# Attention and token mixer on one core: q loaded in 6 KB rows, transposes in row tiles, evictions shared by two engines

## The chip, the cores and the metric

The kernel runs on one core of one Trainium2 chip. The metric is the device time of one execution in microseconds. Before the change the median of three runs was 222.12 us (221.69 to 222.29). Runs of the same kernel come in a fast and a slower state; only fast runs are compared here, and one execution of each kernel carries the profile.

## The reference, cut to what matters

Grouped-query attention (16 query heads, 4 key/value heads, 384 positions, head width 64, 8 batches) followed by a mixer over the positions. Inputs and output are 32-bit floats; the kernel computes in bf16.

```python
k = np.repeat(k, group, axis=1); v = np.repeat(v, group, axis=1)     # group = 4
attn = softmax((1/np.sqrt(D)) * q @ k.transpose(0, 1, 3, 2))
x = (attn @ v).transpose(0, 2, 1, 3).reshape(B, S, H * D)            # 8 x 384 x 1024
wq, wk = x @ w_q, x @ w_k                                            # 64 wide
W_tok = (1/np.sqrt(64)) * np.einsum('bsd,btd->bst', wq, wk)
out = np.maximum(np.einsum('bst,btd->bsd', W_tok, x), 0.0) @ w_out   # 8 x 384 x 1024
```

## The kernel before

A builder writes all engines' instructions in one pass. It keeps estimated clocks for TensorE, VectorE and ScalarE, and at each step it takes the piece of work that those clocks say is ready. What it emits is fixed: if an estimate is wrong, an engine waits.

Per batch: q, k and v are loaded, cast to bf16 on GpSimd, transposed (by TensorE for batches 0 and 1, by DMA afterwards), multiplied to scores, exponentiated on ScalarE and multiplied by v. Then x is transposed and goes through the mixer and the output projection. Positions are dealt out as position = 3 * partition + c, so an output block c of 128 partitions is a store with one stride:

```python
def ld(dst, src, a, z, c0=0, c1=C):                     # C = 3: rows of 3 x 64 floats = 768 bytes
    nc.sync.dma_start(out=dst[:, a:z, c0:c1],
                      in_=src[b, a:z].rearrange("h (p c) d -> p h c d", p=P)[:, :, c0:c1])
...
def x_tr(b, c):                                         # eight 128 x 128 transposes
    ...
    for dc in range(DC):
        nc.tensor.transpose(out=ps[:, dc, :], in_=xn[:, c, dc * P:(dc + 1) * P], identity=ident)
    nc.vector.tensor_copy(out=xTs[b][:, :, c, :], in_=ps)
...
def po():                                               # output projection, one matmul a call
    ...
    osb = osbs[b, c]
    dst = out[b].rearrange("(p c) n -> c p n", c=C)[c]  # 128 rows of 4 KB, one every 12 KB
    ...
        nc.vector.tensor_copy(out=osb[:, n0:n1], in_=ps[:, n0 - half * NH:n1 - half * NH])
    ...
    if half == 1 and not last:
        nc.sync.dma_start(out=dst, in_=osb)             # 512 KB
```

The last store of all is cut into one of 256 KB and two of 128 KB. There are 26 stores in the program.

The softmax here doesn't subtract the row's maximum and nothing guards it: scores larger than these inputs give would overflow.

## Time and profile before

| | before |
|---|---|
| median of the three runs | 222.12 us |
| the profiled execution | 226.12 us, span 224.3 us |
| TensorE busy | 95% of the span |
| last copy of the output ends | 221.54 us in the profile |
| from there to the end | 2.8 us |

Most lines of this profile are in the prediction below. Five more: the shares of the chain that ended last; the DMA queue with its packets, megabytes and share of 16 engines' time; the score matmuls, with busy time, mean ns, and the idle time before them and what ended most of it; and two lines of the DMA issues with count, size and the median time from issue to landing.

```profile
PE 74%; DMA 14%; DVE 3%; SPq 3%; POOL 3%; issue 1%; DVEq 0%
...
q1 hardware_dynamic: 71520, 45.62, 77.6%
...
L259 PE MATMUL sc<-QT,KT 64*128 64x512 bf16 x288 | 47.5, 387 | 3.1 <-DMA QT<-qb 2.9
...
out_dram<-osb SPq DMA_DIRECT2D x23, 512.0 KB, 3.1
...
QT<-qb SPq DMA_TRANSPOSE x18, 3.7
```

Windows: time between the marks, busy time of each engine with the count of instructions, granted TensorE clock, share of the 16 DMA engines (the times of their packets added up, so that it can pass 1), and GB/s.

```profile
215.00:221.50 6.50, 5.74 (x27) 2.41 (x25) 2.80 (x5) 0.00 (x0) 0.00 (x0) 1.00 0.51 202
221.50:224.30 2.80, 0.00 (x0) 0.00 (x0) 0.04 (x1) 0.00 (x0) 0.00 (x0) 1.00 0.28 94
```

The reader is to keep two things: a store lands in 3.1 us, and after the last copy only 2.8 us go by, in which 94 GB/s x 2.8 us = 0.26 MB leave the core.

### The profile page before, as it was taken

The numbers are of one execution on the slowest core, as the hardware profiler recorded it, in microseconds if no ns is written. First come the engines' busy times: TensorE is split into PE (matmuls) and PEld (weight loads), VectorE is DVE, ScalarE is ACT, GpSimd is POOL, SyncE is SP. The second block draws the span as 40 slices with busy tenths as digits, with TensorE's granted clock in tenths as the row PEclk, the third lists the DMA queues.
The fourth block names the chain that finished last, engine by engine and source line by source line (L and its number), as shares of the span: only waits on it lengthen the run. The fifth ranks groups of instructions, "written<-read, shape, count | busy, mean of one in ns | idle before, by whom it ended". The sixth has DMA issues, their size and how long they took to land.

```text
span 224.3 us, 5470 instructions
## 1 busy us (share of the span) xinstructions
PE 214.2 (95%) x2217; PEld 113.6 (51%) x2244; DVE 145.2 (65%) x365; ACT 140.6 (63%) x146; POOL 52.1 (23%) x97
## 2 busy tenths in 40 slices
PE   8999999589999999999999999999999999999993
PEld 5666665245545545454555546554555553434441
DVE  2355786834697758865887648874679569576332
ACT  3599998747788778887887887887888600000000
POOL 1385678406300540045016100620000000000000
PEclk9999999959999999999999999999999999999999
DMA  6996999999399979999999998989224422242424
GB/s 174 324 327 170 410 386 325 136 237 323 65 183 215 335 166 187 222 338 216 223 229 342 154 213 260 281 205 154 99 91 53 143 93 93 93 190 93 180 101 187
DMA packets 71688, 46.09 MB, mean 205 GB/s; under 512 B 42736, under 2 KB 67568, under 8 KB 71664
## 3 DMA queue, kind: packets, MB, share of 16 engines
q1 hardware_dynamic: 71520, 45.62, 77.6%
q8 instruction: 17, 0.28, 0.5%
q10 hardware_dynamic: 144, 0.13, 0.2%
q14 instruction: 7, 0.06, 0.1%
HBM read 23.59 MB, written 12.58 MB: 161 GB/s over the span
## 4 chain that ended last, share of the span: by engine, by line
PE 74%; DMA 14%; DVE 3%; SPq 3%; POOL 3%; issue 1%; DVEq 0%
PE bank L408 37%; PE bank L282 13%; PE sc L259 12%; DMA qraw<-in_q_dram 12%; PE bank L331 4%; SPq L129 3%; PE bank L384 3%; PE bank L362 2%; DMA QT<-qb 2%; PE bank L322 1%; POOL qb L158 1%; DVE osb L421 1%; PE bank L349 1%; DVE msb L389 1%; POOL wqk_sb L596 1%
## 5 line engine op out<-in xcount | busy, mean ns | idle before, releaser
L263 ACT ACTIVATE pt<-sc 128x1024 bf16<-128x1024 f32 x144 | 138.9, 1023 | 34.6 <-PE sc L259 34.4
L408 PE MATMUL bank<-wout_sb,msb 128*128 128x512 bf16 x357 | 91.7, 382 | 1.3 <-issue 0.5
L408 PEld LDWEIGHTS <-msb 128*128 128x128 bf16 x384 | 33.8, 98 | 42.4 <-issue 13.7
L259 PE MATMUL sc<-QT,KT 64*128 64x512 bf16 x288 | 47.5, 387 | 3.1 <-DMA QT<-qb 2.9
L282 PEld LDWEIGHTS <-pt 128*128 128x128 bf16 x1152 | 41.9, 98 | 15.8 <-issue 9.9
L282 PE MATMUL bank<-vext,pt 128*128 128x65 bf16 x1152 | 46.9, 195 | 0.4 <-DVE osb L421 0.2
L421 DVE COPY osb<-bank 128x512 f32<-128x512 f32 (+1 forms) x49 | 33.1, 677 | 21.7 <-PE bank L408 20.5
L289 DVE TENSOR_TENSOR xnat<-bank,rcp 128x256 bf16<-128x256 f32 x96 | 40.8, 425 | 3.3
L389 DVE TENSOR_SCALAR msb<-bank 128x384 bf16<-128x384 f32 x64 | 32.5, 551 | 9.5 <-PE bank L384 9.0
L287 DVE RECIPROCAL rcp<-bank 128x4 f32<-128x4 f32 x96 | 16.9, 176 | 17.6 <-PE bank L282 16.7
L158 POOL CAST qb<-qraw 128x768 bf16<-128x768 f32 x30 | 24.0, 827 | 17.4 <-DMA qraw<-in_q_dram 15.1
L153 POOL CAST kb<-kraw 128x192 bf16<-128x192 f32 x30 | 9.2, 347 | 67.3 <-DMA kraw<-in_k_dram 67.3
L259 PEld LDWEIGHTS <-KT 64*128 64x128 bf16 x288 | 12.4, 94 | 24.1 <-issue 17.2
L117 PE MATMUL bank<-idle 128*128 128x256 bf16 x80 | 14.8, 324 | 1.0 <-DVE idle L562 1.0
L331 PE MATMUL bank<-xT,wqk_sb 128*128 128x384 bf16 x64 | 11.7, 327 | 0.0
L117 PEld LDWEIGHTS <-idle 128*128 128x128 bf16 x80 | 7.9, 114 | 6.6 <-issue 4.0
L384 PE MATMUL bank<-wT,Csb 64*128 64x384 bf16 x32 | 10.6, 332 | 0.4 <-DVE rcp L287 0.3
L384 PE MATMUL bank<-wq,Csb 64*128 64x384 bf16 x32 | 10.6, 332 | 0.0
L599 POOL CAST wout_sb<-wld 128x1024 bf16<-128x1024 f32 x8 | 8.1, 1040 | 4.1 <-DMA wld<-in_moe_w_out_dram 4.1
L366 DVE CAST Csb<-bank 128x512 bf16<-128x512 f32 x8 | 5.5, 688 | 5.2 <-PE bank L362 5.2
L337 DVE CAST wT<-bank 128x384 bf16<-128x384 f32 x8 | 4.5, 558 | 6.7 <-PE bank L331 6.7
L323 DVE COPY xT<-bank 128x1024 bf16<-128x1024 bf16 x10 | 6.9, 688 | 2.5 <-PE bank L322 2.5
(33 smaller groups left out, 70.1 us busy)
## 6 DMA issues: line engine op xcount, KB each, us to landing
out_dram<-osb SPq DMA_DIRECT2D x23, 512.0 KB, 3.1
qraw<-in_q_dram SPq DMA_DIRECT2D x15, 768.0 KB, 7.4
wld<-in_moe_w_out_dram SPq DMA_DIRECT2D x4, 1024.0 KB, 9.5
kraw<-in_k_dram SPq DMA_DIRECT2D x7, 384.0 KB, 4.3
vraw<-in_v_dram SPq DMA_DIRECT2D x7, 384.0 KB, 8.9
qraw<-in_q_dram SPq DMA_DIRECT2D x1, 512.0 KB, 5.3
kraw<-in_k_dram SPq DMA_DIRECT2D x2, 192.0 KB, 3.7
vraw<-in_v_dram SPq DMA_DIRECT2D x2, 192.0 KB, 6.3
```

The source lines that it names most:

```text
L117: nc.tensor.matmul(out=bank_ps[i][:, :256], lhsT=idle[:, :P], rhs=idle, start=True, stop=True)
L158: eng.tensor_copy(out=nats[b][1][:, :, kp, :, u, :].rearrange("p c i d -> p i c d"), in_=raws[b][2][:, h0:h0 + G])
L259: nc.tensor.matmul(out=ps[:, u, :], lhsT=KT[lo:hi, kp * C + kc, :], rhs=QT[lo:hi, t0:t0 + G, :].rearrange("k i p -> k (i p)"), start=True, ...
L263: nc.scalar.activation(out=pt.rearrange("k u i p -> k u (i p)"), in_=ps, func=AF.Exp, scale=attn_scale)
L282: nc.tensor.matmul(out=ps[:, i * DE:i * DE + D + 1], lhsT=tiles[kc][:, u, i, :], rhs=vext[:, 2 * kp + u, kc, :D + 1], start=(kc == 0), sto ...
L287: nc.vector.reciprocal(out=rcp, in_=avv[:, :, D])
L289: nc.vector.tensor_tensor(out=xnats[b][:, c, h0:h0 + G, :], in0=avv[:, :, :D], in1=rcp.to_broadcast([P, G, D]), op=ALU.mult)
L331: nc.tensor.matmul(out=ps, lhsT=wqk_sb[:, dc, :], rhs=xT[:, dc].rearrange("d c p -> d (c p)"), start=(dc == 0), stop=(dc == DC - 1))
L384: nc.tensor.matmul(out=bank_ps[i][:, :S], lhsT=Csb[lo:hi, j * P:(j + 1) * P], rhs=w[lo:hi, :], start=True, stop=True)
L389: nc.vector.tensor_scalar_max(out=msb[:, dc, :], in0=bank_ps[i][:, :S], scalar1=0.0)
L408: nc.tensor.matmul(out=ps, lhsT=msbs[b][:, dc, c * P:(c + 1) * P], rhs=wout_sb[:, dc, half * NH:(half + 1) * NH], start=(nd == 0), stop=(n ...
L421: nc.vector.tensor_copy(out=osb[:, n0:n1], in_=ps[:, n0 - half * NH:n1 - half * NH])
```

## The change

Intent: (1) load q in rows of 6 KB, that is 24 positions of a head, in place of 768 bytes, and get batch 2 ready earlier; (2) do each 128 x 128 transpose on TensorE as two row tiles of 64 rows that run side by side; (3) let the builder's clocks choose VectorE or ScalarE for each copy out of PSUM in the projection and relu; (4) reckon DMA and GpSimd times in the builder too. A partition now holds position = 24 * s + 8 * c + m, so the output store gets another pattern. The core of the diff, cut:

```diff
+    M = 8
+    def evac(dst, src, end, ns_dve, ns_act, relu=False, act=True):
+        late = max(clk["act"], end + 200) + ns_act + MARG
+        if act and late < max(clk["dve"], end + 200) + ns_dve:
+            ...                              # ScalarE: activation Relu, or copy
+        ...                                  # else VectorE
 ... 
-            ld(kraw, k, 0, 4)
-            ld(qraw, q, 0, half)
-            ld(qraw, q, half, Hq)
+            src = q[b].rearrange("(u a) (s t) d -> (a s) u t d", u=2, t=C * M)
+            nc.sync.dma_start(out=qraw[:, :, c0 * M:c1 * M], in_=src[:, :, c0 * M:c1 * M])
 ...
+    def half_trs(srcs):
+        for j, src in enumerate(srcs):
+            for half in range(2):
+                lo, hi = half * H, (half + 1) * H
+                nc.tensor.transpose(out=outs[half][:, j, :], in_=src[lo:hi], identity=ident[lo:hi, lo:hi])
 ...
-            nc.vector.tensor_scalar_max(out=msb[:, dc, :], in0=bank_ps[i][:, :S], scalar1=0.0)
-            ready["M", b, dc] = bank_free[i] = on("dve", 560, end)
+            ready["M", b, dc] = bank_free[i] = evac(msb[:, dc, :], bank_ps[i][:, :S], end, 560, 500, True, True)
 ...
-        dst = out[b].rearrange("(p c) n -> c p n", c=C)[c]
+        dst = out[b].rearrange("(s c m) n -> c m s n", c=C, m=M)[c]
 ...
-            nc.vector.tensor_copy(out=osb[:, n0:n1], in_=ps[:, n0 - half * NH:n1 - half * NH])
+            done = evac(osb[:, n0:n1], ps[:, n0 - half * NH:n1 - half * NH], end,
+                        180 + (n1 - n0), 150 + (n1 - n0) * 0.86, False, True)
 ... (start of the program, order of the first casts, load and casts of batch 2 ahead, x of batch 1 transposed by TensorE and no longer by DMA: cut)
```

The store moves the same 128 rows of 4 KB. As an access pattern it was 128 x 1024; it is now 8 x 16 x 1024.

## The prediction

> **What bounds the kernel now**
>
> I read the page first (busy time, slices), then one table of windows, then the chain of waits, then the timeline where the chain leaves TensorE.
>
> From the page of the kernel before, the slices and three groups:
>
> ```profile
> PE   8999999589999999999999999999999999999993
> ACT  3599998747788778887887887887888600000000
> ...
> PEclk9999999959999999999999999999999999999999
> DMA  6996999999399979999999998989224422242424
> ...
> L263 ACT ACTIVATE pt<-sc 128x1024 bf16<-128x1024 f32 x144 | 138.9, 1023 | 34.6 <-PE sc L259 34.4
> ...
> L117 PE MATMUL bank<-idle 128*128 128x256 bf16 x80 | 14.8, 324 | 1.0 <-DVE idle L562 1.0
> ...
> L322 PE MATMUL bank<-ident,xnat 128*128 128x128 bf16 x80 | 6.1, 220 | 0.0
> ```
>
> TensorE is 90% or more busy in nearly every slice, with one dip near slice 8, where its clock also dips. DMA is full until slice 27. Busy is not useful, though: 80 of the matmuls are fillers on a dummy tile (L117), put in where the builder expected a wait. So I cut the span by phase:
>
> ```profile
> core 0: us, PE busy (x) PEld busy (x) DVE busy (x) ACT busy (x) POOL busy (x), PEclk, DMA share, GB/s
> 0.00:7.10 7.10, 6.06 (x33) 4.20 (x33) 1.82 (x7) 1.69 (x2) 0.91 (x10) 1.00 0.76 204
> 7.10:25.00 17.90, 17.90 (x229) 11.54 (x228) 9.26 (x27) 16.34 (x18) 11.37 (x21) 1.00 0.94 288
> 25.00:35.00 10.00, 10.00 (x152) 6.28 (x150) 7.79 (x21) 9.13 (x10) 6.91 (x7) 1.00 1.04 389
> 35.00:43.20 8.20, 7.47 (x109) 4.16 (x107) 6.78 (x21) 8.11 (x9) 6.34 (x12) 1.00 1.19 220
> 43.20:51.50 8.30, 5.97 (x42) 2.80 (x45) 3.12 (x8) 3.42 (x4) 0.72 (x3) 0.59 1.09 242
> 51.50:177.00 125.50, 123.36 (x1428) 65.47 (x1449) 89.95 (x236) 100.84 (x104) 25.87 (x48) 1.00 0.86 204
> ```
>
> Three regimes. Up to 7.1 us nothing useful can run: the first scores wait for K and q. From 7 to 43 us ScalarE sets the pace (16.34 of 17.9 us busy): 36 exponentials of two batches, one by one. From 43.2 to 51.5 us everything is slack: the granted clock is 0.59, VectorE is busy 3.12 of 8.3 us. From 51.5 us TensorE is the bound.
>
> The chain of waits gives what one instruction costs when they follow each other:
>
> ```profile
> 24.88 14.96 DMA qraw<-in_q_dram
> 39.90 1.60 POOL qb L158 x2
> 41.53 3.79 DMA QT<-qb
> 45.45 0.61 PE sc L259 x2
> ...
> 70.21 0.75 PE bank L282 x24
> ...
> 72.47 0.45 PE bank L322 x8
> ...
> 74.74 1.31 PE bank L331 x8
> ...
> 203.15 8.74 PE bank L408 x40
> ```
>
> The upper part says why 43 to 45 us is empty: batch 2's q was asked for at 24.88 us, arrived at 39.8, was cast, transposed by DMA, and the scores of batch 2 start only at 45.45. The lower part gives pitches: attention 31 ns, a 128-wide transpose 56 ns, projection of x 164 ns, output projection 218 ns.
>
> With these pitches I checked that 51.5 to 170 us has no slack. By source, it holds 100 pairs of score matmuls (x 0.216), 792 attention matmuls (x 0.031), 196 output-projection weight loads (x 0.216), 48 L331, 48 L322, and 18, 15 and 18 of the mixer's pairs and transposes: 21.6 + 24.8 + 42.3 + 7.8 + 2.7 + 7.2 = 106.4 of 118.5 us. The other 12.1 us over 50 bursts of scores is 0.24 us a burst, which is the change into two-row tiling and back. So there a microsecond of TensorE work taken out is a microsecond of time, and nothing else is.
>
> **What the Trainium skill says**
>
> "TensorEngine Tiling (Array Packing)", Key Properties: changing the tiling mode drains TensorE, and tiles run weight loads and matmuls in parallel. The trace agrees with both: 0.24 us a burst above, and four score matmuls of two tiles take 0.61 us together with their four weight loads starting within 0.11 us (timeline).
>
> "TensorE: Matmul & The Clock Gate", Part 1: an idle stretch of some 3.4 us halves the clock until a busy one follows. The trace has one such dip: 2.9 us idle before 45.45, then 0.59 in the window. The single profiled execution took 226.12 us against a median of 222.12, so I take most of the low clock to be this execution's.
>
> "ScalarE: Activation LUTs", What ACT_TABLE_LOAD costs: 186 ns + 0.833 ns an element with immediate scale. That gives 1039 ns for the exponential (measured 1023), so a 128x512 eviction on ScalarE should be about 0.61 us (estimate); VectorE's takes 0.688 us in the trace.
>
> "DMA: Bandwidth & Descriptors", Why a DMA increments its semaphore by 16 and not by 1: a DMA runs on the largest number of engines up to 16 that divides the slowest dimension of both sides. The new output pattern has 8 as its slowest DRAM dimension, so stores may use 8 engines. No run here shows it yet.
>
> **The change part by part**
>
> q in 6 KB rows. A q load of the kernel before is 768-byte runs (256 and 512 bytes for the first). The row becomes 24 consecutive sequence rows of a head, 6 KB. In the windows the queue moved 288 GB/s with q, k and v and 389 GB/s with the weights in 4 KB rows, both with the engines full. 4.7 MB of q for batches 0 to 2 at 389 instead of 288 GB/s: 16.3 - 12.1 = 4.2 us (estimate). Loads and casts of batch 2 also move ahead in program order, behind the weights. Batch 2's q would be there near 36 us; six casts of some 0.5 us and a transpose by DMA (3.7 us to landing) put its first scores near 41 to 42 us, when ScalarE is done with the 36 exponentials. The hole closes. Its worth: 2.9 us idle, 11 fillers (1.4 us) and about 0.41 x 8.3 = 3.4 us of lost clock are 7.7 us in the profiled execution; the timed runs are 4.0 us shorter, so some 3.7 us are left in them. I count 3.0.
>
> Start. ScalarE has holes of 1.06 us at 10.4 and 0.89 us at 34.1, and the first scores wait from 5 to 7.1 us behind a transpose placed by a fixed time and 7 fillers. The new order (all heads of one block, clocks from estimated loads) removes most of this; but q's first piece is 512 instead of 256 KB, and the cast is twice as long. I count 1.0 us.
>
> Row-tiled transposes. Each 128x128 transpose becomes two of 64 rows that run at once, 64 columns wide: at the attention's pitch (65 columns, 31 ns) about 30 ns for the pair instead of 56. x: before 10 blocks of 8, 10 x 0.45 = 4.5 us; after 12 blocks (batch 1 leaves the DMA), 12 x 0.24 = 2.8 us: -1.7 us. The small transposes of wk: 8 x (0.165 - 0.09) = -0.6 us. K and q of batches 0 and 1: 60 x 26 ns = 1.6 us, but these lie in ScalarE's regime and become fillers: I count 0.3. VectorE pays two copies of 0.42 instead of one of 0.69, 0.15 us x 12 = 1.8 us, while it has 28% of its time free: nothing.
>
> ScalarE or VectorE for evictions. VectorE is 72% and ScalarE 80% busy from 51.5 to 177 us, and TensorE was shown to be full. So this frees banks sooner, which almost nobody waits for: 0 there. After 177 us ScalarE is empty, but VectorE is only 56% busy and the forty output projections at 218 ns each show no wait: 0. The last block's two quarter copies (0.42 us each) can go to two engines: -0.35 us.
>
> Output stores. Rows stay 4 KB. If 8 engines carry them, the last 128 KB takes longer by about the time of its bytes, estimated +0.35 us; before that, 512 KB every 3.5 us fits. The two cancel.
>
> Fewer mode changes. x and wk transposes join the row-tiled burst, and tiled steps wait up to 2.0 instead of 1.2 us for the next burst. Most already sat in bursts: 0.
>
> Sum: 3.0 + 1.0 + 1.7 + 0.6 + 0.3 = 6.6 us; 222.1 - 6.6 = 215.5 us.
>
> **Rivals**
>
> The hole moves, not closes. DMA is full until 45 us with the same bytes; if 6 KB rows run no faster, batch 2's q arrives no sooner and the scores still wait. For it: share near 1.0 also when it moved 389 GB/s. Against: that rate itself shows long rows moving more. It would leave 219.
>
> Row tiles don't overlap for short matmuls. If two weight loads per transpose serialise, a pair costs 60 ns: x then costs 12 x 0.48 = 5.8 us instead of 2.8. Against: weight loads of score pairs start together. It would make 218.5.
>
> ScalarE becomes the bound. Evictions of 0.6 us in front of an exponential delay a burst, and TensorE, in fixed order, waits. ScalarE can take some 20% before it is full; the output projection alone is 48 x 0.61 = 29 us. The builder gives VectorE 0.1 us of preference. For a loss: the order comes from estimated clocks, and an error makes waits. It would add 1 to 3 us.
>
> Score matmuls slow down. They now read q in runs of 16 elements with a step between instead of whole rows. If the stream lost 10%, 144 pairs x 22 ns = 3.2 us. No line speaks to it.
>
> More gain than counted: with output projection able to start at about 32 us instead of 49.8 us, the timed runs may recover more than 3.7 us; 212 to 213.
>
> **Range and chances**
>
> The sum's solid part is 2.3 us of transposes; the 4.0 us of the hole and start rest on estimates of DMA, worth 1 to 7. Hence 211.5 to 219.5. Faster by 2% means below 217.7 us: needs two thirds of the sum less a bit, 0.72. Within 2%: 0.25. Slower: needs two rivals at once and no gain, 0.03.
>
> **What would show it**
>
> Right: no idle of TensorE above 1 us after the first scores, PEclk without a dip, output projection starting before 36 us, q loads landing sooner, eight x transposes in 0.24 us in the chain, 12 blocks. Wrong: scores of batch 2 waiting on DMA at 42 us; a pair of half transposes at 56 ns or more; score pairs above 0.23 us; TensorE waiting for ScalarE's evictions or gaps between bursts in 51 to 177 us; a store taking well over 3.1 us to land at the end. Should the fillers of the first 25 us grow by what the transposes save, that part was rightly counted as nothing.

## The result, and the profile after

| | before | after |
|---|---|---|
| median | 222.2 us (221.69 to 224.82, 4 runs) | 232.85 us (231.71 to 234.0, 4 runs) |
| ratio of fast runs | | 1.0454 (95%: 1.0347 to 1.0562), slower |
| span of the profiled execution | 224.3 us | 229.9 us |

A ratio here is the mean time of one kernel's fast runs over that of the other's of the same rounds, so it is not quite the ratio of the medians quoted.

The change costs 10.7 us where 6.6 us of gain had been predicted. The page of the changed kernel, with the lines that answer to those above:

```profile
PE   5999999999999997999999989999599999999950
...
PEclk9799999999999999999999999999889999999996
DMA  6999998939997999989999999999944293344542
...
q1 hardware_dynamic: 54232, 45.10, 84.4%
...
PE 47%; DMA 29%; SPq 5%; ACT 5%; issue 4%; POOL 4%; DVE 1%; POOLq 0%; DVEq 0%; ACTq 0%
...
L294 PE MATMUL sc<-QT,KT 64*128 64x512 bf16 x288 | 47.8, 385 | 5.8 <-DMA QT<-qb 4.2
...
out_dram<-osb SPq DMA_DIRECT2D x23, 512.0 KB
```

The chain's share of TensorE fell from 74% to 47%, and that of DMA rose from 14% to 29%. The queue carries a quarter fewer packets (54,232 for 71,520) and nearly as many bytes, and yet holds the engines longer (84.4% for 77.6%). TensorE has two new dips, in slices 16 and 29 of 40, and the last slice is empty. For the stores the page gives no landing time at all: that field is missing from all its transfers. The chain of waits, middle part (start, length, what):

```profile
82.05 9.05 DMA QT<-qb
...
108.45 5.78 DMA QT<-qb
...
120.19 13.83 DMA vraw<-in_v_dram
...
141.16 12.03 DMA qraw<-in_q_dram
...
156.57 7.46 DMA QT<-qb
...
164.16 0.61 PE sc L294 x4
```

These are links that the chain before did not have after 46 us. The three transposes of q by DMA on this chain take 5.8 to 9.1 us to land; before, the slowest of all 18 took 5.2 us, and the median was 3.7. TensorE waits for it at 91, 114 and 164 us. The windows of the changed kernel:

```profile
7.10:25.00 17.90, 17.71 (x314) 11.12 (x313) 10.95 (x38) 15.96 (x17) 12.92 (x22) 0.90 1.07 372
...
51.50:177.00 125.50, 120.02 (x1384) 62.63 (x1383) 79.78 (x216) 95.62 (x105) 23.84 (x52) 0.99 1.00 195
```

```profile
215.00:222.30 7.30, 6.36 (x30) 2.65 (x28) 0.42 (x1) 2.20 (x5) 0.00 (x0) 1.00 0.50 152
222.30:229.90 7.60, 0.00 (x0) 0.00 (x0) 0.00 (x0) 0.00 (x0) 0.00 (x0) 0.77 0.32 106
```

From 51.5 to 177 us the DMA share is 1.00 (0.86 before) for fewer GB/s (195 for 204), and TensorE is idle for 5.5 us of it (120.02 busy). The 123.36 of the kernel before is no fair measure for this, since its trace lacks 21 matmuls in this window (1,428 for 1,449 weight loads); that of the changed kernel lacks none. At the end there are 7.6 us after the last copy, in which 106 GB/s x 7.6 us = 0.81 MB leave: a store and a half was still to go, where before it was half a store. Just before that, the share stands at 0.50 for 152 GB/s, where before it stood at 0.51 for 202. The trace's single packets tell the two apart: in the changed kernel seven or more are in flight all through this window, and just eight for 6.05 of its 7.30 us. In the kernel before, from 200 us to the last copy, it is none for 11.9 of 21.5 us, and sixteen for 6.1.

The trace has one direct count of how many engines take part: its packets of 4 bytes. There are 2,289 of them before, which is sixteen for each of 67 copies, thirty-two for each of 38 transposes by DMA, and one more. In the changed kernel there are 1,889. With its stores turned back to a pattern of 16 (below) it is 2,097: 208 fewer in the changed kernel, which is 26 stores x 8. So each store ran on 8 engines in place of 16.

The landing times that the page leaves out can be had from the trace's semaphore updates by transfers. There are 1,338, which is nine for each of the 26 stores and sixteen for each of the 69 other transfers. Counted off in the order of issue, the stores take 5.9 to 12.0 us to land (median 7.1; before 1.7 to 8.2, median 2.9), and the transposes of q 3.1 to 9.4 us (median 4.2).

### The profile page after: what moved, and what is told of

Read it like the earlier page. It is cut to its first block, busy times and chain, and to the rows that moved or that the text cites. A ratio compares the mean times of both kernels' runs of the same rounds, so it can differ in the third digit from the quotient of the medians.

```text
span 229.9 us, 5881 instructions
## 1 busy us (share of the span) xinstructions
PE 212.3 (92%) x2409; PEld 110.5 (48%) x2409; DVE 126.7 (55%) x350; ACT 158.0 (69%) x180; POOL 53.3 (23%) x110
## 3 DMA queue, kind: packets, MB, share of 16 engines
q1 hardware_dynamic: 54232, 45.10, 84.4%
## 4 chain that ended last, share of the span: by engine, by line
PE 47%; DMA 29%; SPq 5%; ACT 5%; issue 4%; POOL 4%; DVE 1%; POOLq 0%; DVEq 0%; ACTq 0%
PE bank L441 21%; DMA qraw<-in_q_dram 10%; DMA QT<-qb 10%; DMA vraw<-in_v_dram 9%; PE sc L294 8%; PE bank L319 8%; ACT pt L299 4%; PE bank L145 3%; POOL qb L197 3%; PE bank L365 2%; SPq L234 2%; PE bank L397 1%; PE bank L251 1%; PE bank L418 1%; SPq L176 1%
## 5 line engine op out<-in xcount | busy, mean ns | idle before, releaser
L299 ACT ACTIVATE pt<-sc 128x1024 bf16<-128x1024 f32 x144 | 139.4, 1024 | 38.0 <-PE sc L294 37.6
L441 PE MATMUL bank<-wout_sb,msb 128*128 128x512 bf16 x384 | 96.0, 382 | 0.0
L441 PEld LDWEIGHTS <-msb 128*128 128x128 bf16 x384 | 33.1, 98 | 43.5 <-issue 13.3
L117 DVE TENSOR_SCALAR msb<-bank 128x384 bf16<-128x384 f32 x54 | 27.8, 552 | 15.9 <-PE bank L418 15.7
L197 POOL CAST qb<-qraw 128x512 bf16<-128x512 f32 x45 | 25.9, 619 | 21.9 <-DMA qraw<-in_q_dram 13.1
L119 DVE COPY osb<-bank 128x512 f32<-128x512 f32 (+1 forms) x25 | 16.9, 678 | 24.6 <-PE bank L441 24.3
L114 ACT COPY osb<-bank 128x512 f32<-128x512 f32 (+1 forms) x24 | 13.9, 577 | 19.1 <-PE bank L441 17.4
L145 PE MATMUL bank<-idle 128*128 128x256 bf16 x73 | 13.9, 324 | 1.0 <-DVE idle L617 1.0
L257 DVE COPY xT<-bank 128x512 bf16<-128x512 bf16 x24 | 9.1, 419 | 8.6 <-PE bank L251 8.5
L145 PEld LDWEIGHTS <-idle 128*128 128x128 bf16 x73 | 6.9, 112 | 5.8 <-issue 3.0
```

The costliest lines, as they stand in the source:

```text
L117: nc.vector.tensor_scalar_max(out=dst, in0=src, scalar1=0.0)
L119: nc.vector.tensor_copy(out=dst, in_=src)
L145: nc.tensor.matmul(out=bank_ps[i][:, :256], lhsT=idle[:, :P], rhs=idle, start=True, stop=True)
L197: copy(out=nats[b][1][:, c * M:(c + 1) * M, u, :], in_=raws[b][2][:, u, c * M:(c + 1) * M])
L299: nc.scalar.activation(out=pt.rearrange("k u i p -> k u (i p)"), in_=ps, func=AF.Exp, scale=attn_scale)
L441: nc.tensor.matmul(out=ps, lhsT=msbs[b][:, dc, c * P:(c + 1) * P], rhs=wout_sb[:, dc, half * NH:(half + 1) * NH], start=(nd == 0), stop=(n ...
```

## The experiments

Theory, after the traces: the store's pattern puts it on 8 of the 16 engines. These 8 also carry their share of every load and transpose, and those have landed only when the slowest of their engines is done. The DMA was already nearly full, so transposes come late in the middle, and stores pile up at the end. Rivals: the evictions on ScalarE, put in order by wrong clocks (R1); the scattered order of the rows in DRAM, not the engines (R2); the new loads and transposes, so that the stores only show it (R3).

One warning on correctness: in this reference the rows of a batch are almost alike; rolling them by one position changes the output by 1.3% (relative norm). A store to wrong rows is therefore still told correct. Kernels 2, 3, 5, 9, 11 and 12 put rows in wrong places. The changed kernel, 1, 4, 6, 7, 8 and 10 put them in the right ones by construction.

### 1 to 3: the store's pattern alone

Run 1 keeps everything of the change, but the relu writes its positions in another order, so that the store's outermost dimension is 16. The Trainium skill advises this on "DMA: Bandwidth & Descriptors", Rules for kernel authors: the engines are set by the outermost dimension, which should be a multiple of 16.

```diff
-            ready["M", b, dc] = bank_free[i] = evac(msb[:, dc, :], bank_ps[i][:, :S], end, 560, 500, True, True)
+            ready["M", b, dc] = bank_free[i] = evac(
+                msb[:, dc, :].rearrange("p (c s m) -> p c s m", c=C, m=M),
+                bank_ps[i][:, :S].rearrange("p (c m s) -> p c s m", c=C, m=M), end, 560, 500, True, True)
-        dst = out[b].rearrange("(s c m) n -> c m s n", c=C, m=M)[c]
+        dst = out[b].rearrange("(s c m) n -> c s m n", c=C, m=M)[c]
```

> The changed kernel with the output stores on a pattern whose slowest DRAM dimension is 16 instead of 8 (the relu copies write the rows in that order; right result). Theory S (stores on 8 engines cost both the 4.9 us longer tail and the late transposes of q): tail after the last copy back to about 3 us from 7.6, waits of TensorE on QT near 0, time 213 to 218. Rival T (stores cost only the tail): 227 to 228, waits on QT stay near 4 us. Rival A (clocks and evictions make the waits): as T.

Run 2 keeps the change and takes the old store pattern (wrong rows).

```diff
-        dst = out[b].rearrange("(s c m) n -> c m s n", c=C, m=M)[c]
+        dst = out[b].rearrange("(p c) n -> c p n", c=C)[c]
```

> The changed kernel with only the DRAM rows of the stores changed to those of the kernel before (3 rows apart, one merged dimension of 128); the rows land in the wrong places on purpose. No on-chip instruction differs. Theory S: same as the 16-engine version within 1 us, 213 to 218. Rival T or A: 227 to 228. If this one is fast and the right 16-engine version is not, the permuted relu write is what costs.

Run 3 puts the new store pattern into the kernel before (wrong rows).

```diff
-        dst = out[b].rearrange("(p c) n -> c p n", c=C)[c]
+        dst = out[b].rearrange("(s c m) n -> c m s n", c=C, m=8)[c]
```

> The kernel before with only the DRAM pattern of the stores of the change (slowest dimension 8); wrong places on purpose. Theory S: stores on 8 engines cost here too, tail +4 to +5 us and some waits on QT: 227 to 233. Rival T: about 227. Rival A (the loss is in the change's on-chip part): 222 to 223.

| run | median us | ratio to before (95%) |
|---|---|---|
| 1, change with 16-wide store | 220.42 (219.94 to 221.63) | 0.989 (0.9837 to 0.9944) |
| 2, change with the old store pattern | 219.38 (219.32 to 220.81) | 0.9851 (0.98 to 0.9902) |
| 3, kernel before with 8-wide store | 246.22 (245.97 to 248.97) | 1.1067 (1.0993 to 1.1142) |

The store's pattern is the loss: 232.85 - 220.42 = 12.4 us in the changed kernel, and 246.22 - 222.84 = 23.4 us in the kernel before, which has nothing else of the change. R3 is out. The line of the score matmuls and what they wait for, on the page of run 3:

```profile
L259 PE MATMUL sc<-QT,KT 64*128 64x512 bf16 x288 | 47.9, 391 | 16.3 <-DMA QT<-qb 16.1
```

The same on the page of run 1:

```profile
PE 88%; ACT 5%; issue 2%; DMA 2%; DVE 1%; SPq 0%; DVEq 0%
...
L294 PE MATMUL sc<-QT,KT 64*128 64x512 bf16 x288 | 47.5, 387 | 0.9 <-ACT pt L299 0.3
...
out_dram<-osb SPq DMA_DIRECT2D x23, 512.0 KB, 4.6
```

The wait for the transposed q is gone from run 1 and more than five times the kernel before's 2.9 us in run 3. I had expected run 3 to lose 5 to 11 us; it lost twice as much and more. Runs 1 and 2 missed their range too (213 to 218), by 2.4 and 1.4 us: what the change gains without the loss is less than predicted. Run 2's stores land in 2.9 us and run 1's in 4.6, without a difference in time beyond the intervals: the landing time of a store alone does not tell what it costs.

### 4: the evictions on ScalarE

```diff
-        if act and late < max(clk["dve"], end + 200) + ns_dve:
+        if False and late < max(clk["dve"], end + 200) + ns_dve:
```

> The changed kernel with every eviction on VectorE again, stores still on 8 engines. Theory S: within 1.5 us of the changed kernel, 231 to 234. Rival A (evictions on ScalarE delay exponentials and make the waits): 227 to 229, with the waits of the score matmuls on ScalarE and QT gone.

Measured: 233.35, 234.45 and 235.10 us in its fast runs (a fourth, 238.21, is slow), ratio 1.0526 (1.0456 to 1.0596). Its page still has the wait:

```profile
L294 PE MATMUL sc<-QT,KT 64*128 64x512 bf16 x288 | 48.1, 387 | 4.9 <-DMA QT<-qb 4.5
```

R1 is out: without a single eviction on ScalarE, the kernel is as slow.

### 5 and 9: the number of engines, with the rows equally scattered

Both keep the changed kernel and alter one number of the store's pattern (wrong rows). Run 5 has 16 x 8 x 1024, run 9 has 4 x 32 x 1024.

```diff
-        dst = out[b].rearrange("(s c m) n -> c m s n", c=C, m=M)[c]
+        dst = out[b].rearrange("(s c m) n -> c m s n", c=C, m=16)[c]     # run 5; m=4 in run 9
```

> The changed kernel with the same kind of scattered store rows, but 16 groups of 8 instead of 8 groups of 16 (neighbouring partitions 48 rows apart; wrong places on purpose). Theory S (the number of engines costs): store packets on 16 engines, 218 to 222. Rival R (the scattered row order costs, not the engines): 229 to 233.

> The changed kernel with the slowest dimension of the stores at 4 (wrong places on purpose). Packet times of the changed kernel: stores 863 us, everything else some 2,240 us over 16 engines, 140 us each. Theory L (the loaded engines become the bound of the kernel): 863/4 + 140 = 356 us of packets on each of four engines, time 330 to 370. Rival T (a store is only late, and the tail longer: one store's time doubles again): 240 to 250.

Run 5: 220.02 us (219.89 to 221.18), ratio 0.987 (0.9812 to 0.9929). Run 9: 279.99 us (278.82 to 282.96), ratio 1.2606 (1.2508 to 1.2705). Run 5's rows are as scattered as the change's, and it loses nothing: R2 is out. (The order is not free for the stores themselves: packets of 4 KB take 236 ns on average in runs 1 and 5, and 173 in run 2. The kernel's time does not show it.) With 16, 8 and 4 engines the time is 220.0, 232.9 and 280.0 us; the packets of 4 bytes in run 9 are 1,785, which is 26 x 12 fewer than with 16.

A rival that was not on my list falls with runs 1 and 5 as well: a store of the change holds SyncE's queue, which issues the loads and transposes, for 604 ns, one of run 2 for 333. In runs 1 and 5 it is 557 and 558, and they lose nothing.

Both expectations for run 9 missed, one above and one below. I had taken the times of packets added up per engine as a bound, with 171 us of the weights' packets counted as stores'. Counted rightly for run 9 it is 585/4 + 3,162/16 = 344 us, and the span is 277: packets of one engine overlap, so it is no bound. What the page and the last window of run 9 show:

```profile
L294 PE MATMUL sc<-QT,KT 64*128 64x512 bf16 x288 | 49.1, 394 | 28.7 <-DMA QT<-qb 28.3
```

```profile
257.70:277.00 19.30, 0.00 (x0) 0.00 (x0) 0.00 (x0) 0.02 (x1) 0.00 (x0) 0.58 0.23 90
```

Both symptoms of the change are there, grown: 28.3 us of waiting for transposed q (4.2 with eight engines), and 19.3 us after the last copy (7.6), with a share of 0.23, about four engines of sixteen. The packets of 256 bytes, nearly all of which belong to transposes, got slower too: their mean in the trace is 26.5 ns before, 36.3 ns after and 55.2 ns in run 9, against 23.9, 27.9 and 28.4 ns in runs 2, 1 and 5. A store on fewer engines thus slows transfers that are not stores.

### 11 and 12: which part of the loss is which

If the theory holds, late transposes and the pile at the end are two separate costs. Run 11 takes 16 engines for the last two batches' stores only, run 12 for the first six batches only (both wrong rows).

```diff
-        dst = out[b].rearrange("(s c m) n -> c m s n", c=C, m=M)[c]
+        dst = out[b].rearrange("(s c m) n -> c m s n", c=C, m=16 if b >= 6 else 8)[c]   # run 11
+        dst = out[b].rearrange("(s c m) n -> c m s n", c=C, m=8 if b >= 6 else 16)[c]   # run 12
```

> The changed kernel with only the stores of the last two batches on 16 engines (wrong places on purpose); the stores beside loads and transposes stay on 8. If the loss of 12 us is two separate parts (tail 4.9 us, late transposes 7.3 us): the tail is back at 3 us, the waits on QT stay, 226.5 to 228.5. If the late transposes come from the backlog of the last stores or the tail from the earlier ones: 220 or 232.

> The opposite: the stores of batches 0 to 5 on 16 engines, the last two batches' on 8 (wrong places on purpose). Two parts: waits on QT gone, tail 6 to 8 us, 224 to 226. If the parts are not separate: 220 or 232.

Run 11: two of its six runs, the profiled one among them, are slow; the four fast ones are 227.44, 227.47, 227.82 and 230.84 us, ratio 1.0193 (1.0107 to 1.0279). Run 12: 225.32 us (224.65 to 226.47), ratio 1.0103 (1.0039 to 1.0166). Against run 5, all 16 engines, 220.02 us: eight engines in the first six batches cost 227.6 - 220.0 = 7.6 us, eight in the last two cost 225.3 - 220.0 = 5.3 us. (The rounds of runs 5, 11 and 12 differ; by the ratios it is 7.2 and 5.2 us of 222.5.) Together 12.9 by the medians, and eight throughout cost 232.85 - 220.02 = 12.8. In run 12 the middle is full again, as its window shows:

```profile
51.50:177.00 125.50, 125.47 (x1482) 65.78 (x1480) 84.25 (x230) 100.75 (x110) 25.12 (x54) 1.00 0.91 198
```

TensorE is busy 125.47 of 125.50 us. Its last copy ends at 216.6 us and the span at 223.7: 7.1 us of tail are left. So the two costs add up, as far as intervals of up to 2 us either way can tell.

### 6 to 8: the terms of the prediction, one by one

With the store mended (run 1), two parts of the change are undone, and one is done alone in the kernel before.

Run 6 is run 1 with all evictions on VectorE (the edit of run 4).

> The 16-engine version with every eviction on VectorE. If evictions on ScalarE gained nothing, as predicted: within 1 us of the 16-engine version (219 to 221.5). If they cost (0.5 us ahead of exponentials in the first 45 us, where ScalarE sets the pace): 217.5 to 219. If they gain: above 222.

220.12 us (219.79 to 220.33), ratio 0.9862 (0.9808 to 0.9915), against 220.42 and 0.989: the evictions on ScalarE are worth nothing that these runs can tell; the medians differ by 0.3 us, and the intervals overlap nearly whole.

Run 7 is run 1 with 128-wide transposes for q, K, x and wk.

```diff
-            for half in range(2):
-                lo, hi = half * H, (half + 1) * H
-                nc.tensor.transpose(out=outs[half][:, j, :], in_=src[lo:hi], identity=ident[lo:hi, lo:hi])
-        return outs, two, pe(n * 29.5, "row")
+            nc.tensor.transpose(out=outs[:, j, :], in_=src, identity=ident)
+        return outs, i, pe(n * 56)
 ...                          # one copy instead of two; wk likewise; steps no longer "tiled"
```

> The 16-engine version with the 128-wide transposes of the kernel before. Prediction's term: row tiles are worth 2.3 us (1.7 for x, 0.6 for wk) plus up to 0.6 as 12 blocks stay: 222.5 to 223.5. If row tiles are worth nothing: 220 to 221.

222.51 us (222.24 to 222.67), ratio 0.9969 (0.9915 to 1.0023). Row tiles are worth 222.51 - 220.42 = 2.1 us (the rounds differ: 1.8 by the ratios, and 2.4 against run 6, which has the same rounds). The chain of the changed kernel shows why:

```profile
24.99 0.23 PE bank L251 x16
```

Sixteen half transposes in 0.23 us are 29 ns a pair, where the chain of run 7 has 0.45 us for eight whole ones at the least, 56 ns each.

Run 8 is the kernel before with the load, casts and transposes of batch 2 moved ahead, to close the hole at 43 to 45 us alone.

```diff
+    load(2)                              # after the weights' loads
 ...
+    cast(2)                              # after the weights' casts
 ...
-        if s == 0:
+        if n == 2:
+            if s == 1:
+                start_tr(n)
+            elif 4 <= s < 8:
+                tr_dma(n, s - 4)
+        elif s == 0:
             load(n)
```

> The kernel before with batch 2's loads, casts and transposes moved ahead in the program as in the change, nothing else. Prediction's term for the hole: 3.0 us, part of it from long q rows. If the early place alone closes it: 219 to 220.5. If the hole needs the faster q rows: 221.5 to 223, still with scores waiting on QT near 43 us.

222.79 us (221.88 to 223.64), ratio 0.9994 (0.9918 to 1.0069): no gain. The 3.0 us that I had counted would have been a ratio of 0.987, outside the interval. Its chain shows that the hole is still there:

```profile
23.79 14.93 DMA qraw<-in_q_dram
...
40.40 3.19 DMA QT<-qb
...
43.73 0.39 PE sc L259 x2
```

Batch 2's scores start at 43.73 instead of 45.45 us, still behind a load of 14.93 us; TensorE waits 1.6 us for them, where it waited 2.9. This run keeps the 768-byte rows, so it tests the earlier order, not the rows.

### 10: mending the start

In the changed kernel and in run 1 TensorE has no work from about 4.4 to 6.2 us, and from 7.1 to 25 us the granted clock is 0.90, where the kernel before had 1.00. Run 10 is run 1 with eight more dummy matmuls there.

```diff
     tr_k(0, 0, 1)
+    keep_busy(8 * FILL + 80)
     clk["pe"] = 5200.0
```

> The 16-engine version with 8 more fillers on TensorE while it waits for the first q, so that its clock doesn't drop (0.90 from 7 to 25 us). If the low clock is what made the start 1 us worse instead of better: 1 to 1.5 us off the 16-engine version, 218.5 to 219.5. If ScalarE's pace hides it: 220 to 221.

218.91 us (218.72 to 219.35, 6 runs), ratio 0.9824 (0.9778 to 0.987) to before: the best of all. It is 1.8% faster than the kernel before, just under the 2% that counts as faster here, and its range does not touch run 1's. The chain's shares on its page, and its second window:

```profile
PE 92%; DMA 3%; ACT 1%; DVE 1%; SPq 1%; issue 0%; POOL 0%; DVEq 0%; ACTq 0%
```

```profile
7.10:25.00 17.90, 17.75 (x325) 11.17 (x323) 12.12 (x40) 17.16 (x19) 13.03 (x23) 1.00 1.03 344
```

The clock is 1.00 in this window, ScalarE does 17.16 us of work there in place of 15.96, the two batches of exponentials end near 43.3 us instead of 44.6, and the chain is 92% TensorE.

That the eight matmuls help by way of the clock is likely, but not shown. The 0.90 is one stretch of 3.4 us at half clock, and it depends on the execution: run 9 starts as the changed kernel does, without the extra matmuls, and its profile has full clock in this window.

```profile
7.10:25.00 17.90, 17.71 (x328) 11.29 (x325) 12.09 (x41) 17.26 (x19) 12.40 (x21) 1.00 1.05 354
```

Its two batches of exponentials end at 43.0 us. In the profiles of runs 2, 5, 11 and 12, with the same start, the record of the clock begins only at 9.5 to 12.4 us (the page counts what lies before as full clock), and the exponentials end at 44.4 to 46.3. So an early full clock goes with an early end, but one profile of run 10 cannot tell whether the matmuls bring it about. That its six runs lie within 0.6 us, and the four of run 1 within 1.7, would fit.

## Why the prediction was wrong

**The failed step** is the one on the output stores: "before that, 512 KB every 3.5 us fits. The two cancel." Counted: +0.35 us, set off against a gain. Measured: +12.4 us (the change against run 1), on its own enough to turn the sign. The fact under it was right: the stores do use 8 engines, as the 208 missing packets show. The judgement of what it costs failed in three ways, each with its number:

- I asked whether the stores fit through their engines, and not whom they hold up. The same eight engines carry a share of every load and transpose, and the share of DMA was already 0.86 to 1.19 in my own table of windows from 7.1 us on. Runs 11 and 12 put this part at 7.6 us.
- "Fits" had no margin. 512 KB in 3.5 us are 150 GB/s, and in the last window before the end the stores moved 152 GB/s with eight packets in flight nearly all the time. A backlog made earlier could not be worked off, and 0.81 MB were left at the last copy. Runs 11 and 12 put this part at 5.3 us.
- The sign of it stood in my list of what would show me wrong ("a store taking well over 3.1 us to land at the end"), and it came: 5.9 us at the least. But no rival and no part of the range was made of it, so the range (211.5 to 219.5) could not hold the result.

**The hole and the start** were predicted at 4.0 us together. Run 1 is 2.4 us faster than before (220.42 for 222.84), of which row tiles are 2.1 and evictions 0, so 0.3 us is left for both; run 10's start makes it 1.8. The traces divide the 0.3. The first 36 exponentials end at 44.54 us in run 1 and at 43.55 before, so the start lost 1.0 us where 1.0 was to be gained. The gap from there to batch 2's first exponential is 1.34 us and was 2.61, so the hole gave 1.3 us where 3.0 were counted. The hole's size came from a profiled execution in the slow state. I took 4.0 us off for that and still counted 3.0; in the fast profile of run 3, which is the kernel before but for the stores (the first at 59.6 us), TensorE waits there for 1.2 us and not 2.9, and run 8, whose profile has full clock throughout, gained nothing by moving the work ahead. For the start, the prediction saw the dummy matmuls that would go and not that TensorE would then stand idle for 1.8 us; putting eight back is worth 1.5 us (run 1 to run 10).

**Right in kind:** row-tiled transposes, by the pitch that was predicted (30 ns a pair, 29 found). The size agrees less well than 2.6 us counted and 2.1 measured look. The sum set two more blocks of x against the gain (and took 12 x 0.24 for 2.8, it is 2.9); run 7 has twelve blocks as run 1 has, for which the same count gives 12 x 0.21 + 0.6 + 0.3 = 3.4 us. Batch 2's q lands at 36.0 us in run 1 (39.9 before), as counted ("near 36"), and no score waits for it there. That the long rows themselves load faster does not show: from batch 3 on, the q of a batch takes 8.0 to 11.4 us to land in run 1 and 7.7 to 8.4 in run 2, and took 7.8 to 9.4 before. Evictions on ScalarE, 0 counted in the middle, 0 found. The rival that score matmuls slow down did not come true: they take 385 ns on average, 387 before. The rivals "row tiles don't overlap" and "ScalarE becomes the bound" fell with runs 7 and 6. The output projection starts at 39.9 us in the changed kernel and at 50.0 before: earlier, but not before 36 us, as the list had it.

**What stays open.** Run 3 lost 23.4 us by the store pattern that cost the change 12.4. Its q rows of 768 bytes hold the DMA longer (the packets of q, k and v add up to some 1,000 us of engine time before and 850 in the change), which would leave less room; no run separates this. Run 1's stores take 4.6 us to land and run 2's 2.9, at the same number of engines; run 5's scattered ones take 4.5, so it goes with the pattern, but why is not known. Which 8 of the 16 engines carried the stores cannot be seen, since the kept packets have no engine's number. And the prediction's 0.24 us a burst for the change of tiling is a remainder of its sum, which no run tested.

## What to carry to other kernels

When a layout changes, look at the outermost dimension of every transfer on both sides, not only at row length: here the same 128 rows of 4 KB cost 220, 233 or 280 us of kernel time at 16, 8 or 4. A transfer on part of the DMA engines is judged by what else waits on these engines, so where the DMA share is near 1 (0.86 here before the change), "its bandwidth suffices" is no argument. If the layout needs the narrow pattern, try to mend the order in a copy that is made anyway, as the relu did in run 1 at no cost beyond the intervals.

## What the Trainium skill lacked or had wrong

- "DMA: Bandwidth & Descriptors": the rule for the number of engines agrees with the count (208 fewer packets of 4 bytes for 26 stores). It has no figure for what fewer engines cost in a kernel whose DMA is busy: 12.4 us of 220 at eight engines and 60 us at four, with transposes of q by DMA that took up to 9.4 us to land, where 5.2 was the longest before.
- The same page does not say, for this chip, how long a transfer occupies the queue that issues it, by pattern: a store took SyncE's queue 333 ns with the pattern of 128 x 1024, 558 ns with 16 x 8 x 1024 and 604 ns with 8 x 16 x 1024. Run 5 shows no cost of the 558 ns.
- "TensorEngine Tiling (Array Packing)": that tiles run independently holds for transposes of 64 rows by 128 columns too: 29 ns a pair against 56 ns for a whole one, worth 2.1 us here. The page names a theoretical speedup of up to two for a dimension of 64; the trace gives 56 / 29 = 1.9, and the page has no figure for transposes.
- "TensorE: Matmul & The Clock Gate": it ties a halved clock to an idle stretch of some 3.4 us. In the profiles of the changed kernel and of run 1, some 1.8 us without work in the first 7 us were followed by 3.4 us at half clock; in that of run 9, with the same gap, they were not. The page has no figure for how much idle time is enough when it is shorter than that stretch.
